# Storing a transposed activation by blocks, loading q in smaller pieces, and new due times for a hand-planned order

## The chip, the cores and the metric

The kernel runs on one core of one Trainium2 chip. The metric is the device time of one execution in microseconds (us). Before the change the median of eight runs was 908.71 us (907.18 to 910.9).

Names used here: TensorE (PE in the profile; PEld are its weight loads), VectorE (DVE), ScalarE (ACT), GpSimd (POOL), and SyncE (SP), which issues nearly all DMAs. All 16 DMA engines serve one queue here.

## The reference

Linear attention without softmax, then an MLP with softplus. All inputs are float32 in the reference; the weights arrive as 64-bit floats.

```python
kv  = einsum('bhsd,bhse->bhde', k, v)            # 8 batches, 8 heads, 576 rows, 64 wide
out = einsum('bhsd,bhde->bhse', q, kv)
rms = sqrt(mean(out * out, axis=-1) + 1e-6)
x   = (out / rms * g_norm) -> 4608 tokens x 512
h   = x @ w_in                                   # 512 -> 2048
y   = softplus(h) @ w_out                        # 2048 -> 512
```

## The kernel before, in words

**Tiles and blocks.** The 4608 tokens are 36 tiles of 128 rows; three tiles are a block of 384 tokens, so there are 12 blocks. A batch of 576 tokens is four and a half tiles.

**Attention part of a tile** (`rows`, L508): q is turned so that the head dimension lies on the partitions; `out_rows` (L521, PE) multiplies it with the batch's kv; ACT squares (L590), DVE sums by head (L525), POOL takes the power -1/2 (L528, L529), DVE scales (L533). The first two batches' q is turned by PE (L577) and copied by ACT (L584); from batch 2 on DVE turns it in 32x32 blocks (L552) from a tile `qa` that `load_q` (L413) fills with four transfers a batch (L423). `kv_of` (L473) loads k and v (L491, and the rows that are left over into `tail` tiles, L489) and multiplies them on PE (L502) in five steps a batch; ACT copies the result (L505).

**x^T.** For the first twelve tiles (`BY_PE`), PE turns the normalized x (L539) and ACT copies the result from PSUM to a tile of ring `m` (L599); SP stores it in DRAM as x^T, one tile a store, 512 rows of 512 bytes (L600). For the later tiles DVE turns x in blocks into a tile of ring `xb` (L616), and a block is stored at once in four stores (L620). The DRAM copy x^T has one tensor of 512 x 384 for each block.

**Split.** For an exact float32 product in the fast format each number is split in three parts: ACT makes the high part (L445), DVE the two others (L448, L452), into `xv`. The tiles of blocks 0 and 1 (`AT_ONCE`) are split straight from PSUM; from block 2 on `x_again` loads x^T back (L638) and splits that. The weights are converted from 64-bit words on DVE and ACT (L294 to L324) and divided in three parts as well (`divide`, L356 to L378); for the first four chunks PE makes the last remainder (L374, L375: a pair).

**MoE part.** d_ff is cut in 16 chunks of 128. A step is one chunk for one block: `mm1` (12 matmuls, L660), softplus (L682, L684) and its split (L671, L675), `mm2` (L667, three times three matmuls, one for each tile). The steps run in three phases over all 12 blocks: phase 0 takes 4 chunks for blocks 0 to 3 and 6 for the others. Partial sums go to DRAM at the end of a phase (ACT, L703; stored by L724) and come back in the next (L707, added in L709). 192 steps in all.

**The order.** Every operation is a task with an engine, a cost in ns, a due position (`pos`, in steps) and the ring places that it takes and gives back. `Plan.order` (L69) simulates engines, rings and one DMA queue and takes, engine by engine, the ready task with the smallest position among those that could start first. The program is written in that order, so each engine's order is fixed at build time; at run time each engine works through its list and waits on semaphores. While PE has nothing to do before step 6, the planner inserts filler matmuls (`warm`, L778). SP works in order as well: a store that waits for its data holds the loads behind it.

Due positions come from the list `P0` (L190): `CONVERT` and `FETCH` (when the weights of the first four chunks are converted and fetched), `EARLY` (the attention tasks, the loads of x, of partial sums) and `LATER` (the other chunks).

**Rings** (L217): `m` has 13 places, `qa` and `xb` one, `tp` one PSUM bank, `o` two. A place is free again when the last reader of its tile is done; for a stored tile that is when the store has landed.

Of the kernel before, what the change touches and what calls it, by code (L numbers as in the profile page):

```python
# [18 lines left out]
P = 128  # L19
# [21 lines left out]
class Plan:  # L41
# [15 lines left out]
    def slot(self, ring):  # L57
        return Slot(ring)

    def add(self, engine, ns, run, after=(), pos=0.0, take=(), give=(), size=0, behind=None, follows=None):  # L60
        t = Task(engine, ns, run, [a for a in after if a is not None], pos, list(take), list(give), size)
        for s in t.give:
            s.readers += 1
        self.tasks.append(t)
        t.follows = follows
        t.behind = behind
        return t
# [79 lines left out]
def kernel(  # L147
# [24 lines left out]
    nc = tc.nc  # L172
    B, H, S, D = q.shape
# [3 lines left out]
    NP = H // 2  # L177
    KD, KF = d_model // P, d_ff // P
    NT = 384
    TB = NT // P  # L180
# [6 lines left out]
    PLACES = 8  # L187
    LAST = PHASES[-1]

    P0 = [-93.0, 0.8, -33.3, -5.7, -14.1, 1.5, -43.9, 2.2, -65.0, -42.8, -62.7, -19.7, -30.7, -6.2,  # L190
          -2.2, -4.7, 2.5, -26.5, 18.0, 10.5, 5.5, 8.5, -2.0, 2.5, 3.5, 25.5, -16.5, 10.0, 6.5, 41.0,
          52.0, 65.5, 54.5, 72.0, 91.5, 94.5, 115.5, 106.0, 111.5, 8.5]
    CONVERT, FETCH, EARLY, LATER = P0[:8], P0[8:16], P0[16:27], P0[27:]
    BY_PE = 12
    AT_ONCE = 2 * TB
# [27 lines left out]
    slot, add = plan.slot, plan.add  # L223

    def new(s, shape, dtype=F32):
        if s.ring == "o":
            s.tile = o_banks[:, :, s.place]
            return s.tile
        pool = ps if s.ring in PS else sb
        s.tile = pool.tile(shape, dtype, tag=f"{s.ring}_{s.place}", name=f"{s.ring}_{s.place}")  # L230
        return s.tile
# [172 lines left out]
    xd = [dram.tile([d_model, NT], F32, name=f"x{n}") for n in range(n_blocks)]  # L404
    xb_slots = {}
    x_there = {}
# [3 lines left out]
    BL = 32  # L410
    q_slots, q_loads = {}, {}

    def load_q(b):  # L413


        q_slots[b], q_loads[b] = slot("qa"), []
        pos = x_pos(first_tile[b] + 1) - EARLY[7]

        def run(e, c):
            if not (e or c):  # L420
                new(q_slots[b], [P, NP * S])
            r0 = BL * (2 * e + c)
            nc.sync.dma_start(  # L423
                out=q_slots[b].tile[r0:r0 + BL].rearrange("j (i d) -> j i d", d=BL),
                in_=q[b, e * NP:(e + 1) * NP, :, BL * c:BL * (c + 1)].rearrange("p (i j) d -> j (p i) d", j=BL))

        for e in range(2):
            for c in range(2):
                q_loads[b].append(add("SP", 450, lambda e=e, c=c: run(e, c), (), pos + 0.2 * (2 * e + c),
                                      [q_slots[b]] if not (e or c) else [], [], 2190, behind=int(pos) - 3,  # L430
                                      follows=q_loads[b][-1] if e or c else None))

    def split(ph, t, x, ready, pos):
        n, i = divmod(t, TB)
        if i == 0:
            xv_slots[ph, n] = slot("xv")
        dst = xv_slots[ph, n]

        def cols(m, dtype=F32):
            if dst.tile is None:  # L440
                new(dst, [P, 3, KD, NT], F32R)
            return (dst.tile if dtype == F32R else dst.tile.bitcast(F32))[:, m, :, i * P:(i + 1) * P]

        def high():
            nc.scalar.activation(cols(0, F32R), x.tile, func=AF.Identity, scale=g_down)  # L445

        def low():
            nc.vector.scalar_tensor_tensor(out=cols(1, F32R), in0=x.tile, scalar=g_col, in1=cols(0),  # L448
                                           op0=ALU.mult, op1=ALU.subtract)

        def less():
            nc.vector.scalar_tensor_tensor(out=cols(2, F32R), in0=cols(1), scalar=-RADIX, in1=cols(0),  # L452
                                           op0=ALU.mult, op1=ALU.add)

        before = x_split.get((ph, n), [None])[-1:]
        a = add("ACT", 700, high, [ready] + ([] if i == 0 else [first_high[ph, n]]), pos, [dst] if i == 0 else [])
        if i == 0:
            first_high[ph, n] = a
        b = add("DVE", 740, low, [a], pos, [], [x])
        c = add("DVE", 700, less, [b], pos)  # L460
        x_split.setdefault((ph, n), []).append(c)
# [6 lines left out]
    def x_pos(t):  # L468

        n = t // TB  # L470
        return t * EARLY[0] + EARLY[1] if n == 0 else first_step[0, n] - (EARLY[2] if n == 1 else EARLY[3]) + t % TB
# [35 lines left out]

    def rows(t):  # L508
        pos = x_pos(t)
        tp, qT, o, x, r, xp, xg = (slot(n) for n in ("tp", "m", "o", "x", "r", "tp" if t < AT_ONCE else "o", "m"))  # L510

        def out_rows():

# [27 lines left out]
        def part_of_qT(n, r0):  # L541
            if qT.tile is None:
                new(qT, [P, NP, P])
            return qT.tile[:, :, r0:r0 + n]

        turned = []
        for b, r0, n, s0 in parts(t):
            if b >= 2:
                if b not in q_slots:
                    load_q(b)  # L550
                turned.append(add(
                    "DVE", 690 if n == P else 420, lambda b=b, r0=r0, n=n, s0=s0: nc.vector.transpose(  # L552
                        out=part_of_qT(n, r0),
                        in_=q_slots[b].tile.rearrange("k (p s) -> k p s", p=NP)[:, :, s0:s0 + n]),
                    q_loads[b], pos - 1, [qT] if not r0 else [], [q_slots[b]], follows=turned[-1] if turned else None))
                continue
# [17 lines left out]
            def turn_q(n=n, q_s=q_s, at_qa=at_qa, tp=slot("tp" if t < AT_ONCE else "o")):  # L574
                y = new(tp, [P, NP, P])
                for p in range(NP):
                    nc.tensor.transpose(y[:, p, :n], pairs(natural(q_s, at_qa)[:n], p), ident[:n, :n])  # L577

            tp = turn_q.__defaults__[-1]
            ld = add("SP", 900, load, (), pos - EARLY[7], [q_s] if not at_qa or t == 0 else [], [], 1220 * n // P,  # L580
                     behind=int(pos) - 3, follows=first_load[0] if t and at_qa else None)
            first_load.append(ld)
            a = add("PE", 440, turn_q, [ld], pos - 1, [tp], [q_s])
# [3 lines left out]
        a = o_task = add("PE", 640, out_rows, turned + need, pos, [o], [qT])  # L587
        for pt in parts(t):
            o_tasks.setdefault(pt[0], []).append(a)
        a = add("ACT", 600, lambda: nc.scalar.activation(new(x, [P, H, D]).rearrange("s (a k) d -> s a (k d)", k=2), o.tile, func=AF.Square,  # L590
                                                              scale=D ** -0.5), [a], pos, [x])
        a = add("DVE", 690, reduce, [a], pos, [r])
        a = add("POOL", 2300, root, [a], pos)
        a = add("DVE", 700, norm, [a, o_task], pos, [], [o, r])
        if t < BY_PE:
            a = add("PE", 440, turn_x, [a], pos + 0.5, [xp], [x])
            if t < AT_ONCE:
                split(0, t, xp, a, pos + 0.5)
            a = add("ACT", 600, lambda: nc.scalar.copy(new(xg, [P, KD, P]), xp.tile), [a], pos + 1, [xg], [xp])  # L599
            x_there[t] = [add("SP", 450, lambda: nc.sync.dma_start(  # L600
                out=x_of(t), in_=xg.tile), [a], pos + 1, [], [xg], 1000)]
            return


# [1 line left out]
        n, i = divmod(t, TB)  # L606
        g = TB if n < n_blocks - 1 else 1
        i0, i = i - i % g, i % g
        if i == 0:
            xb_slots[n] = slot("xb"), []  # L610
        xb, turns = xb_slots[n]
# [18 lines left out]
    def x_of(t):  # L630

        n, i = divmod(t, TB)
        return xd[n][:, i * P:(i + 1) * P].rearrange("(a p) t -> p a t", p=P)
# [120 lines left out]
    for c in range(KF):  # L754
        for j in (2 * c, 2 * c + 1):
            pos = CONVERT[j] if c < 4 else LATER[c - 4] + LATER[12] * (j % 2)
            weight(j, pos, FETCH[j] if c < 4 else pos)
    for b in range(B):
        kv_of(b)
        for t in range(n_tiles):  # L760
            if parts(t)[-1][0] == b:
                rows(t)
# [51 lines left out]
```

## Time and profile before

| | us |
|---|---|
| median of eight runs | 908.71 |
| the profiled execution, its own time | 909.08 |
| span of the profiled execution | 907.3 |
| PE busy | 893.4 |
| DVE busy | 624.2 |
| ACT busy | 408.1 |
| the 192 x 12 matmuls of L660 | 435.3 |
| the 192 x 9 matmuls of L667 | 433.5 |
| stores of x^T by tiles (L600), issue to landing, median of 12 | 4.1 |
| loads of q for DVE (L423), issue to landing, median of 24 | 6.8 |

The time of an execution is a little longer than its span in the trace. Busy times of different engines lie beside each other. In the page's 40 slices, one digit is the busy share of a slice of 22.7 us in tenths. In a table by windows the columns are the window, its length, then each engine's busy time with the number of its instructions, the granted TensorE clock as a share of full speed, the share of the 16 DMA engines' time that packets took, and GB/s. The chain of waits is read in order of time: start, length and what ran then; a DMA in it is a piece of time in which the engine waited for that transfer.

### The profile page before, as it was taken

The numbers are of one execution on the slowest core, as the hardware profiler recorded it, in microseconds if no ns is written. First come the engines' busy times: TensorE is split into PE (matmuls) and PEld (weight loads), VectorE is DVE, ScalarE is ACT, GpSimd is POOL, SyncE is SP. The second block draws the span as 40 slices with busy tenths as digits, with TensorE's granted clock in tenths as the row PEclk, the third lists the DMA queues.
The fourth block names the chain that finished last, engine by engine and source line by source line (L and its number), as shares of the span: only waits on it lengthen the run. The fifth ranks groups of instructions, "written<-read, shape, count | busy, mean of one in ns | idle before, by whom it ended". The sixth has DMA issues, their size and how long they took to land.

```text
span 907.3 us, 15563 instructions
## 1 busy us (share of the span) xinstructions
PE 893.4 (98%) x5983; PEld 789.0 (87%) x5983; DVE 624.2 (69%) x1054; ACT 408.1 (45%) x788; POOL 84.7 (9%) x79
## 2 busy tenths in 40 slices
PE   7989999999999999999999999999999999999998
PEld 5678888888888899998998989999899999989996
DVE  6887988676567877888668787886534555555553
ACT  4766555443444555644435454554323333333331
POOL 0443222122213200000000000000000000000000
PEclk8999999999999999999999999999999999999999
DMA  9999987579672626364334544740330433333323
GB/s 241 271 210 278 257 171 227 115 174 190 184 150 62 149 94 186 105 198 151 105 128 128 174 142 142 249 146 20 105 105 1 139 105 105 105 105 105 104 73 102
DMA packets 211451, 131.58 MB, mean 145 GB/s; under 512 B 102320, under 2 KB 185264, under 8 KB 211376
## 3 DMA queue, kind: packets, MB, share of 16 engines
q1 hardware_dynamic: 211216, 130.58, 53.0%
q8 instruction: 47, 0.77, 0.4%
q14 instruction: 28, 0.23, 0.1%
q10 hardware_dynamic: 160, 0.00, 0.0%
HBM read 91.75 MB, written 38.80 MB: 144 GB/s over the span
## 4 chain that ended last, share of the span: by engine, by line
PE 95%; DMA 3%; ACT 0%; DVE 0%; SPq 0%; issue 0%; DVEq 0%
PE h L660 45%; PE s L667 44%; DMA m<-in_v_dram 2%; PE o_banks L521 2%; PE tp L502 2%; PE h L778 1%; PE s L502 1%; DMA m<-in_k_dram 0%; PE o_banks L539 0%; PE tp L577 0%; DVE xv L448 0%; PE tp L539 0%; PE h L374 0%; SPq L491 0%; ACT m L599 0%
## 5 line engine op out<-in xcount | busy, mean ns | idle before, releaser
L660 PE MATMUL h<-xv,w 128*128 128x384 f32 x2304 | 435.3, 337 | 0.2 <-ACT w L378 0.2
L667 PE MATMUL s<-w,gv 128*128 128x512 f32 x1728 | 433.5, 395 | 0.0
L660 PEld LDWEIGHTS h<-xv,w 128*128 128x128 f32 x2304 | 406.3, 188 | 16.4 <-ACT w L378 0.4
L667 PEld LDWEIGHTS s<-w,gv 128*128 128x128 f32 x1728 | 319.8, 188 | 60.4 <-DVE gv L675 0.2
L682 ACT ACTIVATE g<-h 128x384 f32<-128x384 f32 x192 | 94.2, 491 | 401.2 <-PE h L660 399.4
L671 DVE TENSOR_TENSOR gv<-g,gv 128x384 fp32r<-128x384 f32 x192 | 106.5, 555 | 180.5 <-ACT gv L684 179.5
L684 ACT ACTIVATE gv<-g 128x384 fp32r<-128x384 f32 x192 | 100.7, 524 | 24.7 <-PE s L667 18.5
L675 DVE SCALAR_TENSOR_TENSOR gv<-gv 128x384 fp32r<-128x384 f32 x192 | 106.7, 556 | 5.8
L448 DVE SCALAR_TENSOR_TENSOR xv<-m,g_col,xv 128x512 fp32r<-128x512 f32 x102 | 76.0, 745 | 2.5 <-ACT xv L445 2.4
L452 DVE SCALAR_TENSOR_TENSOR xv<-xv 128x512 fp32r<-128x512 f32 x108 | 74.3, 688 | 2.5
L445 ACT ACTIVATE xv<-m,g_down 128x512 fp32r<-128x512 f32 x102 | 70.1, 712 | 2.9 <-DMA m<-x 2.8
L529 POOL TENSOR_TENSOR r<-r,half 128x8 f32<-128x8 f32 x36 | 66.1, 1835 | 3.0
L709 DVE SCALAR_TENSOR_TENSOR m<-s,scale,m 128x512 f32<-128x512 f32 x24 | 17.9, 747 | 29.7 <-PE s L667 29.7
L533 DVE TENSOR_TENSOR x<-o_banks,r 128x512 f32<-128x512 f32 x36 | 24.8, 689 | 18.8 <-POOL r L529 8.4
L528 POOL TENSOR_SCALAR r<-r 128x8 f32<-128x8 f32 x36 | 17.3, 480 | 216.4 <-DVE r L525 215.9
L709 DVE SCALAR_TENSOR_TENSOR m<-s,m 128x512 f32<-128x512 f32 x36 | 23.7, 685 | 7.8 <-PE s L667 7.8
L521 PEld LDWEIGHTS o_banks<-kv,m 64*64 64x64 f32 x1152 | 19.9, 134 | 9.7 <-issue 5.5
L311 ACT ACTIVATE sq<-sq,big 128x512 bf16<-128x512 bf16 x32 | 22.9, 715 | 10.7 <-DVE m L307 10.7
L359 DVE TENSOR_TENSOR m<-m,w 128x512 f32<-128x512 f32 x30 | 20.6, 687 | 10.2 <-ACT w L356 9.8
L525 DVE TENSOR_REDUCE r<-x 128x8 f32<-128x512 f32 x36 | 24.2, 678 | 4.6 <-ACT x L590 4.6
L590 ACT ACTIVATE x<-o_banks 128x512 f32<-128x512 f32 x36 | 21.1, 592 | 12.3 <-PE o_banks L521 7.0
L521 PE MATMUL o_banks<-kv,m 64*64 64x64 f32 x1152 | 24.5, 224 | 0.8 <-ACT m L584 0.7
(71 smaller groups left out, 429.7 us busy)
## 6 DMA issues: line engine op xcount, KB each, us to landing
m<-x SPq DMA_DIRECT2D x102, 256.0 KB, 4.7
part<-m SPq DMA_DIRECT2D x72, 256.0 KB, 2.6
m<-part SPq DMA_DIRECT2D x72, 256.0 KB, 4.0
raw<-in_moe_w_in_dram SPq DMA_DIRECT2D x16, 512.0 KB, 5.7
m<-in_k_dram SPq DMA_DIRECT2D x32, 256.0 KB, 5.0
m<-in_v_dram SPq DMA_DIRECT2D x32, 256.0 KB, 4.7
raw<-in_moe_w_out_dram SPq DMA_DIRECT2D x16, 512.0 KB, 5.7
qa<-in_q_dram SPq DMA_DIRECT2D x24, 288.0 KB, 6.8
```

The source lines that it names most:

```text
L445: nc.scalar.activation(cols(0, F32R), x.tile, func=AF.Identity, scale=g_down)
L448: nc.vector.scalar_tensor_tensor(out=cols(1, F32R), in0=x.tile, scalar=g_col, in1=cols(0), op0=ALU.mult, op1=ALU.subtract)
L452: nc.vector.scalar_tensor_tensor(out=cols(2, F32R), in0=cols(1), scalar=-RADIX, in1=cols(0), op0=ALU.mult, op1=ALU.add)
L521: nc.tensor.matmul(y[r0:r0 + P // 2, a, c0:c0 + D], lhsT=qT.tile[e * D:(e + 1) * D, p, r0:r0 + P // 2], rhs=kvs[b % 2][e * D:(e + 1) * D, ...
L529: nc.gpsimd.tensor_tensor(out=r.tile, in0=r.tile, in1=half, op=ALU.pow)
L660: nc.tensor.matmul(hp, lhsT=w_in.tile[:, i, kd * P:(kd + 1) * P], rhs=xv.tile[:, i, kd], start=(m == 0), stop=(m == 3 * KD - 1))
L667: nc.tensor.matmul(mine[i].tile, lhsT=gv.tile[:, m, i * P:(i + 1) * P], rhs=w_out.tile[:, m], start=(c == cs[0] and m == 0), stop=(c == cs ...
L671: nc.vector.tensor_tensor(out=gv.tile[:, 1], in0=g.tile, in1=gv.tile.bitcast(F32)[:, 0], op=ALU.subtract)
L675: nc.vector.scalar_tensor_tensor(out=gv.tile[:, 2], in0=f32[:, 1], scalar=-RADIX, in1=f32[:, 0], op0=ALU.mult, op1=ALU.add)
L682: a = add("ACT", 490, lambda: nc.scalar.activation(new(g, [P, NT]), h.tile, func=AF.Softplus, scale=1.0 + E), [a], s, [g], [h])
L684: a = add("ACT", 530, lambda: nc.scalar.activation(new(gv, [P, 3, NT], F32R)[:, 0], g.tile, func=AF.Copy, scale=DOWN), [a], s, [gv])
L709: a = add("DVE", 700, lambda: nc.vector.scalar_tensor_tensor(out=new(ot, [P, d_model]), in0=bank.tile, scalar=(scale if ph == LAST else 1. ...
```

## The change

For the first twelve tiles ACT now copies a tile's x^T into its third of a block's tile of ring `xb`, and when the third tile is copied SP stores the block at once: 512 rows of 1536 bytes. All three tiles' readers wait for that one store. `load_q` loads a batch's q in eight transfers (two of the four heads of a partition group each) instead of four; the planner's cost of one is 500 ns of SP and 1095 of the queue instead of 450 and 2190. The list of due positions has other values: among them the first four chunks' conversions, where the attention tiles of block 0 stand (`EARLY[0]`, `EARLY[1]`), kv of batch 0 (`EARLY[5]`), the loads of x (`EARLY[9]`) and of partial sums (`EARLY[10]`).

In the changed file L600 is L612, L599 is L608, L638 is L652, L660 is L674, L667 is L681, L671 and L675 are L685 and L689, L778 is L792.

```diff
-    P0 = [-93.0, 0.8, -33.3, -5.7, -14.1, 1.5, -43.9, 2.2, -65.0, -42.8, -62.7, -19.7, -30.7, -6.2,
-          -2.2, -4.7, 2.5, -26.5, 18.0, 10.5, 5.5, 8.5, -2.0, 2.5, 3.5, 25.5, -16.5, 10.0, 6.5, 41.0,
-          52.0, 65.5, 54.5, 72.0, 91.5, 94.5, 115.5, 106.0, 111.5, 8.5]
+    P0 = [-74.0, 0.3, -15.3, -11.7, -11.1, 1.5, -22.9, 2.2, -78.5, -42.8, -76.2, -17.2, -26.2, -5.2,
+          -0.2, -4.2, 1.5, -19.5, 14.0, 10.5, 5.5, 25.5, -2.0, 2.5, 3.5, 2.5, -45.5, 7.5, 6.5, 38.5,
+          52.0, 65.5, 54.5, 72.5, 91.0, 94.5, 114.5, 110.5, 111.0, 8.5]
...
-        def run(e, c):
-            if not (e or c):
+        def run(a, p):
+            if not (a or p):
                 new(q_slots[b], [P, NP * S])
-            r0 = BL * (2 * e + c)
+            e, c = divmod(a, 2)
             nc.sync.dma_start(
-                out=q_slots[b].tile[r0:r0 + BL].rearrange("j (i d) -> j i d", d=BL),
-                in_=q[b, e * NP:(e + 1) * NP, :, BL * c:BL * (c + 1)].rearrange("p (i j) d -> j (p i) d", j=BL))
-
-        for e in range(2):
-            for c in range(2):
-                q_loads[b].append(add("SP", 450, lambda e=e, c=c: run(e, c), (), pos + 0.2 * (2 * e + c),
-                                      [q_slots[b]] if not (e or c) else [], [], 2190, behind=int(pos) - 3,
-                                      follows=q_loads[b][-1] if e or c else None))
+                out=q_slots[b].tile[BL * a:BL * (a + 1), p * S:(p + 2) * S].rearrange("j (i d) -> j i d", d=BL),
+                in_=q[b, e * NP + p:e * NP + p + 2, :, BL * c:BL * (c + 1)].rearrange("p (i j) d -> j (p i) d", j=BL))
+
+        for a in range(4):
+            for p in range(0, NP, 2):
+                q_loads[b].append(add("SP", 500, lambda a=a, p=p: run(a, p), (), pos + 0.1 * (2 * a + p // 2),
+                                      [q_slots[b]] if not (a or p) else [], [], 1095, behind=int(pos) - 3,
+                                      follows=q_loads[b][-1] if a or p else None))
...
-            a = add("ACT", 600, lambda: nc.scalar.copy(new(xg, [P, KD, P]), xp.tile), [a], pos + 1, [xg], [xp])
-            x_there[t] = [add("SP", 450, lambda: nc.sync.dma_start(
-                out=x_of(t), in_=xg.tile), [a], pos + 1, [], [xg], 1000)]
+            n, i = divmod(t, TB)
+            if i == 0:
+                xb_slots[n] = slot("xb"), []
+            xb, turns = xb_slots[n]
+
+            def copy():
+                if i == 0:
+                    new(xb, [P, KD, NT])
+                nc.scalar.copy(xb.tile[:, :, i * P:(i + 1) * P], xp.tile)
+
+            turns.append(add("ACT", 600, copy, [a], pos + 1, [] if i else [xb], [xp], follows=turns[-1] if turns else None))
+            if i == TB - 1:
+                st = add("SP", 450, lambda: nc.sync.dma_start(
+                    out=xd[n].rearrange("(a p) t -> p a t", p=P), in_=xb.tile), turns, pos + 1, [], [xb], 2280)
+                for u in range(t - i, t + 1):
+                    x_there[u] = [st]
```

More of the change, by code (lines that the diff above doesn't have):

```diff
@@ L509, in rows @@
         pos = x_pos(t)
-        tp, qT, o, x, r, xp, xg = (slot(n) for n in ("tp", "m", "o", "x", "r", "tp" if t < AT_ONCE else "o", "m"))
+        tp, qT, o, x, r, xp = (slot(n) for n in ("tp", "m", "o", "x", "r", "tp" if t < AT_ONCE else "o"))
         def out_rows():
```

## The prediction

> **What bounds the kernel now.** I read the page first, then busy time by windows, then TensorE's waits, then the chain of waits between 48 and 71 us. Page:
>
> ```profile
> span 907.3 us, 15563 instructions
> PE 893.4 (98%) x5983; PEld 789.0 (87%) x5983; DVE 624.2 (69%) x1054; ACT 408.1 (45%) x788; POOL 84.7 (9%) x79
> ...
> DMA  9999987579672626364334544740330433333323
> ```
>
> TensorE (PE) is busy 98% of the span, and the DMA engines are full only in the first five slices, some 113 us. The windows (busy PE, PEld, DVE, ACT, POOL, then clock, DMA share, GB/s) say where PE is not busy:
>
> ```profile
> 0.00:40.00 40.00, 33.13 (x377) 22.60 (x377) 29.85 (x54) 23.61 (x45) 10.64 (x15) 0.91 0.96 255
> 40.00:66.00 26.00, 23.61 (x291) 19.45 (x289) 22.30 (x39) 19.04 (x39) 7.91 (x9) 1.00 1.00 224
> 66.00:98.00 32.00, 31.89 (x392) 27.15 (x389) 25.24 (x43) 18.93 (x37) 13.37 (x11) 1.00 1.03 251
> 98.00:320.00 222.00, 222.00 (x2007) 192.46 (x2007) 165.69 (x282) 105.16 (x203) 52.81 (x46) 1.00 0.72 167
> 320.00:902.80 582.80, 582.80 (x2926) 527.31 (x2924) 380.32 (x639) 241.38 (x466) 0.00 (x0) 1.00 0.39 120
> ```
>
> From 98 to 902.8 us PE never idles, so nothing there can be won, only lost. The first matmul group of the MoE part (L660) starts at 40.00; behind it PE idles 2.39 + 0.11 = 2.5 us until 98, and runs six filler matmuls of L778 (rows at 59.09, 59.91 and 71.89 us: 0.62 + 0.71 + 0.63 = 2.0). So 4.5 us is all that a better order after step 0 can recover. PE's waits and the chain say what the idle is:
>
> ```profile
> PE s L502 <- DMA m<-in_v_dram: 4.3, 3, 3.6
> PE tp L502 <- DMA m<-in_v_dram: 2.0, 2, 1.3
> ```
>
> ```profile
> 48.48 7.34 DMA m<-in_v_dram
> 55.82 0.04 issue
> 55.86 0.69 PE tp L502 x16
> ...
> 58.63 6.67 DMA m<-in_v_dram
> 65.29 0.14 issue
> 65.43 0.69 PE tp L502 x16
> 66.11 2.29 PE h L660 x12
> 68.40 0.61 PE tp L502 x16
> 69.02 0.62 PE o_banks L521 x32
> 69.64 0.58 PE tp L539 x4
> 70.22 0.70 PE s L667 x3
> ```
>
> The kernel waits for v, 6.7 to 7.3 us after its issue, while the DMA share is 1.00: **the start is a DMA queue with TensorE behind it**, the rest is TensorE. The last rows are my prices for PE: 0.62 us for a kv step (L502) and a tile's q·kv (L521), 0.45 for four transposes (L539), 0.70 for a third of L667, 2.1 for an L660 group.
>
> **The change, part by part.**
>
> *Stores of x^T.* Twelve stores of 256 KB in 512-byte rows become four of 768 KB in 1536-byte rows. The trace's DMA records from 60 to 130 us give 30.5 ns for a 512-byte packet, 52.7 for 1024, 104.4 for 2048, so some 78 for 1536. A tile cost 512 x 30.5 / 16 = 0.98 us of all 16 engines, a block will cost 512 x 78 / 16 = 2.5 instead of 2.93: 1.7 us less queue over four blocks. ScalarE (ACT) makes the same twelve copies (0.58 each). Twelve places of the 13-place ring m are no longer taken, and SP issues eight DMAs fewer.
>
> *q.* Six batches, four transfers of 288 KB each, become eight of 144 KB, with the same 128-byte packets: 9216 x 14.0 / 16 = 8.1 us of queue a batch, as before. SP issues 24 more, at least 0.46 us each (the shortest row of L423), 11 us over 210; the longest rows of L423 are 5.3 and 5.9 us, when one transfer held SP, and shorter ones let other loads in between. In the built order each SP DMA waits on one of eight semaphores in turn, last used eight DMAs earlier, so eight are in flight: eight pieces are 8 x 1.0 us of work against the 2.0 us in which the fastest store (L724) lands. I take 0; bounds -1 (the hole that one long issue leaves) to +1 (SP late once).
> A q transfer of 288 KB lands in 4.7 to 9.4 us at a full DMA share, so its fixed part is covered. The Trainium skill, "DMA: Bandwidth & Descriptors", section Bandwidth, speaks against this edit: batch transfers to 1 MiB or more. By the 2 us a transfer that its section "Anatomy of one DMA" fits for the software queue, 24 more would be 48 us, 6 with eight in flight, and the time 913.5; the full queue speaks for 0.
>
> *The due times (P0).* They set the order of every engine up to about 120 us, and here the time is decided. The first 25 rows of SP's order are equal, so both kernels stand alike up to the v load that lands at 32.15 (PE waits for it until 32.17). From there I price both queues with the records above: k and v 1.69, a weight 1.69, a tail 0.63, a tile of q 1.27, a 144 KB piece 1.01, a partial sum 0.84. Check on before: w_in of chunk 3 comes after 22.1 us of queue and landed at 54.87 (22.7 measured, x1.03); a later v after 31.3, landed 65.3 (x1.06); the last x load of block 2 after 57.4, landed 89.8 (x1.00). So my sums hold within 0 to 6%; I use 1.03.
>
> Step 0: in both orders 10 L502, 4 L521, 3 L539, 6 L577 and 3 weight pairs stand before it, and 47 against 46 fillers. The third tile's chain (L533 at 36.08, L539 at 36.91, L445, copy, L448 at 38.81, L452 until 40.28) is the same. After puts the pair of w_in chunk 2 (0.75) right ahead of it: 40.8. That pair stood earlier in before's idle; at step 2 the two orders differ by 0.2 us.
>
> Step 3 (last of block 0): in after w_in of chunk 3 stands behind 26.4 us of queue, because of four pieces of batch 2's q, block 0's store and w_out ahead of it: 32.15 + 1.03 x 26.4 = 59.3, 4.4 us later than before. From landing to the last ACT division before took 7.9 us; after has 0.4 us more of VectorE (DVE) ahead in its order and a split and a copy on ACT (1.1): 59.3 + 9.4 = **68.7** against 66.04. But by then after's PE has done two thirds of L667, two L502 and two L539 more: 1.4 + 1.24 + 0.9 = 3.5 us. Even is 69.5: after is 0.8 ahead.
>
> Block 2's first step: before at 96.4. After has three L667 thirds, one L502 and two L521 more ahead of it: 2.1 + 0.62 + 1.24 = 4.0, even is 100.4. Before spent 0.7 on the way for the fillers at 71.89 and small idles that after's order has not (its six fillers, 2.0, all stand before step 3): after comes to 98.9. Block 2's last x load is behind 62.9 us of queue: 96.9 at x1.03, ready 2.2 later (L445, L448, L452), 99.1. It just fits.
>
> *The new wait.* Ring xb has one buffer: a block's first copy waits until the previous block's store has landed. On ACT behind it stand the divisions of w_out chunk 3 and the squares of tiles 8 and 9, and on PE tile 8's and 9's L521, which need the two o banks that the uncopied tiles hold. Block 1's store is behind 40.3 us: lands 73.7. PE reaches that L521 at 68.7 + 2.1 + 0.6 + 2.1 = 73.5, and the copy takes 0.6: 0.8 late, part of which PE would wait anyway for the next v load (41.8 us of queue, 75.2). Ends 0 and 0.8; I take 0.3. Block 2's store (55.9 us, 89.7) meets the next copy at about 88 with PE's L521 1 us behind it: 0 to 1, I take 0, for two thirds of L667 stand between.
>
> Sum: -0.8 - 0.7 + 0.3 = **-1.2 us**. From block 4's first step on both PE orders have done the same work, so nothing else comes in. The profiled run is 909.08 (span 907.3 and 1.8 around it), 0.4 above the median of the eight runs: 907.9 for such a run, **907.5** on the median.
>
> **Rivals.**
> 1. *The order holds better* (17%): L667, L502 and L521 cover every DMA wait, the fillers fall into time that PE would lose anyway, and shorter issues of q close the queue's hole before 65 us. All 2.5 us idle go, with up to 1.5 of the fillers: -2.5 to -4, some 905.5. For it: 1.7 us less queue. Against: w_in chunk 3 arrives later.
> 2. *The store's landing takes over* (slower, 28%). If the queue runs at x1.06 or SP meets one more wait, block 1's store lands at 75, block 2's at 91.4, block 2's last x load at 98.8 (ready 101.0, 2.1 after PE), block 3's store (70 us of queue) at 106.4 in front of VectorE's first block turn, with a step's L671 and L675 behind it. It decides from 2 us of delay at 95 us of the span: -1.2 + 2.1 + 1 + 0.5, or about +2.4, 911. For it: DMA share 1.00 to 1.03 and a lead of 0.8 to 1.5 us only. Against: the x1.00 measured at 90 us.
> 3. *The idle only moves* (13%): w_in chunk 3 at x1.06 is 60.1, step 3 at 69.5, even; PE waits for a weight instead of v: 0 (-0.5 to +1.5), 908.7.
>
> **How the numbers follow.** Forecast 42% (-2.5 to -0.3). A measurement tells about 0.2%, 1.8 us, from no change: faster than 906.9 is rival 1 and less than half of the forecast, 0.37; slower than 910.5 is most of rival 2 and a little of 3, 0.28; the rest 0.35. The range, 905.0 to 911.3, reaches to both rivals.
>
> **What would show it.** First L660 at 40.5 to 41; step 3 at 68 to 69.5 with its releaser ACT (division), not v; PE idle between 40 and 98 under 1.5 us; no idle ahead of block 2's step; fillers again 2 us; a block's store landing in 5 to 7 us; waits of ACT on a landing store ahead of the copy (L608) under 1 us. Wrong if PE idles after 98 us, if L608 waits 2 us or more, or if the first L660 starts after 42.

## The result, and the profile after

The changed kernel takes 911.35 us (median of 11 runs, 910.92 to 914.16) against 908.42 for the kernel before on the same chip (30 runs): a ratio of 1.0035, 95% interval 1.0028 to 1.0043. It is slower by about 3 us. Its profiled execution took 911.53 us, 2.45 more than that of before.

The page of the changed kernel:

```profile
span 909.7 us, 15578 instructions
PE 894.2 (98%) x5982; PEld 788.5 (87%) x5982; DVE 625.9 (69%) x1054; ACT 409.2 (45%) x788; POOL 82.3 (9%) x79
...
DMA  9999889479682535355333435651330433433323
```

The same windows as for before (length, then busy PE, PEld, DVE, ACT, POOL, clock, DMA share, GB/s):

```profile
0.00:40.00 40.00, 31.82 (x374) 21.82 (x374) 29.27 (x53) 23.20 (x44) 8.85 (x15) 0.91 1.00 254
40.00:66.00 26.00, 25.10 (x309) 20.09 (x308) 20.99 (x36) 17.23 (x36) 7.82 (x7) 1.00 0.99 234
66.00:98.00 32.00, 31.03 (x372) 25.81 (x369) 26.28 (x45) 22.10 (x45) 11.77 (x12) 1.00 1.07 263
98.00:320.00 222.00, 220.43 (x2000) 190.71 (x1999) 166.84 (x281) 102.96 (x196) 53.89 (x47) 1.00 0.71 163
320.00:902.80 582.80, 582.80 (x2929) 528.04 (x2928) 379.36 (x638) 243.72 (x470) 0.00 (x0) 1.00 0.39 120
```

TensorE's idle time between 40 and 66 us fell from 2.39 to 0.90 us. In its place stand 0.97 us between 66 and 98 (0.11 in before), and 1.57 after 98, where before had none. What TensorE waited for has changed too:

```profile
PE o_banks L521 <- DVE x L533: 0.9, 1, 0.9
PE o_banks L577 <- ACT x L590: 0.9, 1, 0.9
...
PE o_banks L521 <- ACT xb L608: 0.7, 1, 0.7
...
PE o_banks L539 <- DVE x L533: 0.5, 1, 0.5
```

The 2.0 us on v (row `PE tp L502` of before) are gone. All but the last of the rows shown are waits at `o_banks`, the PSUM tile that holds both places of ring `o`; the last, L539 behind L533, waits for the x that it turns. The longest stretch stands right ahead of block 2's first step; the chain of waits there reads:

```profile
98.80 0.45 PE o_banks L539 x4
99.25 0.02 issue
99.27 0.59 ACT xb L608
99.87 0.04 issue
99.91 0.74 PE o_banks L521 x32
100.65 0.02 issue
100.67 0.60 ACT x L590
...
101.37 0.70 DVE x L533
102.07 0.04 issue
102.11 0.69 PE o_banks L521 x32
```

TensorE turns tile 11 (L539), ACT copies it out of its place (L608), TensorE can write tile 13 into that place (L521), ACT squares it (L590), VectorE divides tile 12 (L533), which frees the other place, and TensorE writes tile 14 (L521). Six operations of three engines, one after the other, with no transfer among them. Block 2's first step follows at 102.74.

To see what was lost where, I compared the starts of the 192 steps in both traces and took off the difference in the work that TensorE had done by then. After is 0.64 us late at step 0; 0.06 at step 6; 0.63 at step 7; 2.53 at step 8, which is block 2's first; 3.0 from step 16 to the last step (the end itself is 2.5 late, because what follows the last step is 0.6 shorter). From step 0 to step 16 both kernels do exactly the same work on TensorE (192 matmuls of the first product, 135 of the second, 448 of L521 and so on): 98.93 us before, 101.29 after. Of these 2.36 us, 0.94 are more idle time; 1.42 are rows of the same work taking longer until the next one starts, above all the 36 matmuls of L539 (3.91 to 4.58) and the 135 of L681 (33.19 to 33.68). For L539 the traces show why: the 27 transposes that another one follows take 3.16 us in before and 3.17 in after; the nine that end a tile go from 0.76 to 1.41. A row of a step or a filler starts 0.03 us after the last transpose has started, L521, L502 or L577 0.11 us or more after it, and one of those three follows six times in after and three times in before. So this part, too, is the order.

### The profile page after: what moved, and what is told of

Its sections match the earlier page's. It is cut to its first block, busy times and chain, and to the rows that moved or that the text cites. A ratio compares the mean times of both kernels' runs of the same rounds, so it can differ in the third digit from the quotient of the medians.

```text
span 909.7 us, 15578 instructions
## 1 busy us (share of the span) xinstructions
PE 894.2 (98%) x5982; PEld 788.5 (87%) x5982; DVE 625.9 (69%) x1054; ACT 409.2 (45%) x788; POOL 82.3 (9%) x79
## 4 chain that ended last, share of the span: by engine, by line
PE 96%; DMA 2%; ACT 1%; DVE 0%; issue 0%; SPq 0%; DVEq 0%
PE s L681 45%; PE h L674 45%; PE o_banks L521 2%; PE tp L502 2%; DMA m<-in_v_dram 1%; PE h L792 1%; DMA m<-in_q_dram 1%; PE s L502 1%; DMA tail<-in_k_dram 0%; PE o_banks L539 0%; DVE x L533 0%; PE tp L577 0%; PE h L374 0%; PE tp L539 0%; PE o_banks L577 0%
## 5 line engine op out<-in xcount | busy, mean ns | idle before, releaser
L674 PE MATMUL h<-xv,w 128*128 128x384 f32 x2304 | 435.0, 337 | 0.0
L681 PE MATMUL s<-w,gv 128*128 128x512 f32 x1728 | 434.9, 395 | 0.0
L674 PEld LDWEIGHTS h<-xv,w 128*128 128x128 f32 x2304 | 406.5, 188 | 15.9
L681 PEld LDWEIGHTS s<-w,gv 128*128 128x128 f32 x1728 | 319.5, 188 | 60.6 <-DVE gv L689 0.2
L685 DVE TENSOR_TENSOR gv<-g,gv 128x384 fp32r<-128x384 f32 x192 | 106.5, 555 | 180.9 <-ACT gv L698 179.5
L689 DVE SCALAR_TENSOR_TENSOR gv<-gv 128x384 fp32r<-128x384 f32 x192 | 106.9, 557 | 5.9
L529 POOL TENSOR_TENSOR r<-r,half 128x8 f32<-128x8 f32 x36 | 65.1, 1809 | 3.0
L533 DVE TENSOR_TENSOR x<-o_banks,r 128x512 f32<-128x512 f32 x36 | 24.7, 686 | 15.3 <-POOL r L529 6.9
L521 PEld LDWEIGHTS o_banks<-kv,m 64*64 64x64 f32 x1152 | 19.9, 134 | 11.5 <-issue 5.8
L590 ACT ACTIVATE x<-o_banks 128x512 f32<-128x512 f32 x36 | 21.1, 593 | 14.9 <-PE o_banks L521 6.5
L521 PE MATMUL o_banks<-kv,m 64*64 64x64 f32 x1152 | 24.6, 224 | 2.4 <-DVE x L533 0.9
```

What stands on the lines that cost most here:

```text
L521: nc.tensor.matmul(y[r0:r0 + P // 2, a, c0:c0 + D], lhsT=qT.tile[e * D:(e + 1) * D, p, r0:r0 + P // 2], rhs=kvs[b % 2][e * D:(e + 1) * D, ...
L529: nc.gpsimd.tensor_tensor(out=r.tile, in0=r.tile, in1=half, op=ALU.pow)
L674: nc.tensor.matmul(hp, lhsT=w_in.tile[:, i, kd * P:(kd + 1) * P], rhs=xv.tile[:, i, kd], start=(m == 0), stop=(m == 3 * KD - 1))
L681: nc.tensor.matmul(mine[i].tile, lhsT=gv.tile[:, m, i * P:(i + 1) * P], rhs=w_out.tile[:, m], start=(c == cs[0] and m == 0), stop=(c == cs ...
L685: nc.vector.tensor_tensor(out=gv.tile[:, 1], in0=g.tile, in1=gv.tile.bitcast(F32)[:, 0], op=ALU.subtract)
L689: nc.vector.scalar_tensor_tensor(out=gv.tile[:, 2], in0=f32[:, 1], scalar=-RADIX, in1=f32[:, 0], op0=ALU.mult, op1=ALU.add)
```

## The experiments

The theories, as the expectations name them: **A**, the store by blocks costs, through its one buffer; **B**, the due times cost, or fit only one combination; **C**, q in eight pieces costs or gains. **D** came later: any order other than that of before costs some microseconds. A ratio is to the kernel before, timed on the same chip in the same session, with its 95% interval.

### One part of the change at a time

Each kernel is the one before with one part of the diff alone (`f_store`, `f_q`, `f_due`), or with both data edits and the old due times (`f_data`). `g_no_store` and `h_no_q` are the changed kernel without one data edit. The edits in short:

```diff
 f_store  + xb.tile[:, :, i*P:(i+1)*P] / one store a block      (rest as before)
 f_q      + for a in range(4): for p in range(0, NP, 2)          (rest as before)
 f_due    + P0 = [-74.0, 0.3, -15.3, ...]                        (rest as before)
 f_data   - P0 = [-74.0, ...]   + P0 = [-93.0, ...]              (rest as after)
 g_no_store  - one store a block   + one store a tile            (rest as after)
 h_no_q      - for p in range(0, NP, 2)   + for c in range(2)    (rest as after)
```

> The kernel before with the block stores of x^T alone (old q transfers, old due times). Theory A, the one-buffer ring: a block's copies are ordered behind the landing of the store before, the turned tiles hold the two o banks and the next tiles' L521 start late: 910.5 to 912, PE idle of 1.5 us or more between 85 and 110 us. Theory B, the due times make the loss: 907.5 to 909.5. Theory C, the q pieces make it: as before, 908 to 909.

> The kernel before with q in eight pieces a batch alone. Theories A and B: within 1 us of before, 907.5 to 909.5. Theory C: 910.5 to 912.

> The kernel before with the new due times alone: stores by tiles from ring m, q in four transfers. Theory A: within 1 us of before or faster, since a copy waits for no store. Theory B: 910.5 to 912, with step 3 at about 71 us as in the changed kernel. Theory C: as A.

> The changed kernel with the old due times: block stores and q pieces. Theory A: 910.5 to 912. Theory B: 907.5 to 909.5. Theory C: 910.5 to 912.

> The changed kernel without the block stores: q in eight transfers and the new due times, x^T stored by tiles as before. Theory A (the store costs the 3 us): 907 to 909. Rival B (the due times fit only with the block store, which frees twelve places of ring m and saves queue time): 912 to 916, near the 914.4 of the due times alone.

> The changed kernel with q in four transfers as before: block stores in the one-buffer ring and the new due times. If the due times fit the block store, it comes near the changed kernel: 910 to 913. If they fit only both edits together, as the run without the block store suggests: 914 to 920.

| | due times of before | new due times |
|---|---|---|
| no data edit | 908.42 | `f_due` 914.42, 1.0072 [1.0045, 1.0099] |
| q in eight | `f_q` 909.07, 1.0006 [0.9991, 1.0021] | `g_no_store` 915.78, 1.0077 [1.0054, 1.0099] |
| stores by blocks | `f_store` 922.79, 1.0154 [1.0118, 1.0191] | `h_no_q` 913.31, 1.0060 [1.0038, 1.0082] |
| both | `f_data` 917.50, 1.0097 [1.0066, 1.0128] | after 911.35, 1.0035 [1.0028, 1.0043] |

Of the first four runs only `f_q` lies in a range that a theory gave for it; `f_store`, `f_due` and `f_data` lie above all of theirs. `g_no_store` is in B's range, `h_no_q` between its two (four runs, 911.3 to 915.8). TensorE's order in `h_no_q` is that of after, row by row, and its interval overlaps after's, so these runs don't show that q in eight pieces is worth anything beside the other two parts.

No part is worth a fixed sum: the store by blocks costs 14 us with the old due times and, with the new ones, saves 4 beside q in eight (915.78 to 911.35). The new due times cost 6 us alone and save 6 beside both data edits. So B holds in this form: what the due times cost or save depends on the edits beside them. `f_q` shows a second thing. At step 3 it is 2.7 us ahead of before, with the difference in work taken off, and the lead is gone between steps 26 and 27, where the chain of waits of `f_q` has batch 5's last piece:

```profile
186.23 5.31 DMA qa<-in_q_dram
...
191.83 0.46 DVE m L552
192.29 0.04 issue
192.33 1.29 PE o_banks L521 x62
```

VectorE waits for that piece to land, and TensorE for VectorE.

### Is it the one buffer?

The weights of chunks 6 and 7 have places of 6 KB a partition, the size of `xb`, and are not there yet while blocks 0 to 3 are stored. First, each of the four blocks takes such a place, and the planner makes its own order for it (the lines that matter):

```diff
-    BY_PE = 12
+    BY_PE, OWN = 12, ["w0_6", "w1_7", "w0_7", "w1_6"]
...
-                xb_slots[n] = slot("xb"), []
+                xb_slots[n] = slot(OWN[n]), []
```

> The kernel before with block stores only (922.8 us with the one-buffer ring), but each of the first four blocks has a buffer of its own: the places of the weights of chunks 6 and 7, which are free until chunk 6 and 7 are converted late in phase 0. Theory A (the ring of one buffer makes the loss: a copy waits until the block before has landed, and behind it ACT, the o banks and PE): the loss goes, 907 to 910. Rival B (the loss is the store itself: tiles become readable only when the third is copied, and 512 rows of 1536 bytes go out in one burst): still 918 to 923.

> The changed kernel, with four buffers for the first four blocks as in the run beside it. Theory A: the 1.9 us that the chain of copies on the o banks costs between 94 and 103 us go, and some of the 3 us stays away: 908 to 909.5. Rival B (the due times were fitted to the one-buffer ring, so a different ring leads the planner to another order that fits no better): 910 to 914.

> The kernel before with both data edits (block stores and q in eight transfers), the old due times, and a buffer of its own for each of the first four blocks. With one buffer it took 917.5 us. Theory A (the ring of one buffer makes most of that): 908 to 911. Rival (two changes of order add up): 913 to 917.

Measured: `g_store_own` 910.64 (1.0030 [1.0015, 1.0045]) against 922.79 with one buffer; `h_data_own` 912.19 (1.0051 [1.0032, 1.0071]) against 917.50; `g_all_own` 910.32 (1.0023 [1.0012, 1.0033]) against 911.35. The one buffer makes 12 of `f_store`'s 14 us, more than half of `f_data`'s 9 and perhaps 1 of after's 3 (there the intervals overlap). `g_store_own` is 0.6 over A's range, `h_data_own` between its two ranges, `g_all_own` in B's. For the first two that reads as A, but it doesn't say how. So the second pair keeps the planner's order for one buffer, instruction by instruction, and only writes to the other memory, so that no copy can wait for a landing store:

```diff
                 if i == 0:
-                    new(xb, [P, KD, NT])
+                    xb.tile = sb.tile([P, 3, d_model], F32R, tag=OWN[n], name=OWN[n])
```

> The changed kernel with its order unchanged on every engine, but the first four blocks are written to memory of their own (the places of the weights of chunks 6 and 7), so no copy waits for a landing store. If the wait for the one buffer at run time makes the 3 us: 908 to 909.5. If it is the order that the planner built around the one buffer (the copy of a turned tile put behind the store, the o bank held meanwhile): 910.5 to 911.5, no gain.

> The kernel before with block stores only, in the order that took 922.8 us with the one-buffer ring, but with memory of its own for each of the first four blocks. With this order kept, a wait at run time for the buffer would be gone: 911 to 915 if that wait was the cost (a copy waited 2.1 us there, and TensorE up to 7 us). If the order is the cost: 919 to 923; the planner's own order for four buffers took 910.6.

Measured: `i_all_order_kept` 912.11 (1.0037 [1.0024, 1.0050]), no different from after. `i_store_order_kept` 921.38 (1.0135 [1.0112, 1.0157]), no different from `f_store`, where ACT's waits had one row for the buffer:

```profile
ACT xb L608 <- DMA x<-xb: 2.1, 1, 2.1
```

That wait is gone in `i_store_order_kept`. Its median is 1.4 us lower, with overlapping intervals, and its trace is 2.4 us shorter from step 0 to step 16 (110.21 against 112.60), so the wait can have cost `f_store` some 2 us. **The rest of the loss, some 11 us, is the order that the planner builds around the buffer:** with the same edit and the same memory, its order for four buffers takes 910.64. In after no row of ACT waits for a landing store at all, so `i_all_order_kept` had no wait to remove, and its time stays. A as a wait at run time falls as the main cost.

### The data edits in the order of before

Here every engine keeps the order of before. `h_q_same_order` issues each of q's transfers as two halves; `i_both_order_of_before` also stores blocks 0, 1 and 3 whole, from memory of their own (two loads of block 2 stand ahead of its last store in SP's order, so block 2 stays with tiles). The edits, shortened:

```diff
+            for p in range(0, NP, 2): nc.sync.dma_start(
+                out=q_slots[b].tile[r0:r0 + BL, p * S:(p + 2) * S]..., in_=q[b, e * NP + p:e * NP + p + 2, ...]...)
...
+        elif not left[n]:      # the block's third tile
+            nc.sync.dma_start(out=xd[n].rearrange("(a p) t -> p a t", p=P), in_=xt_of(whole[n]))
```

> The kernel before with its own order on every engine, each of the four transfers of a batch's q issued as two of 144 KB one behind the other. It takes the size of the pieces apart from the other order that they lead the planner to. If the pieces themselves win (a long issue no longer holds SP): 905.5 to 907.5, and step 3 before 65 us. If only the order made the 2.6 us of the run with q in eight pieces: 908 to 909.5.

> The order of the kernel before on every engine, with q's transfers issued in halves (907.6 alone) and with blocks 0, 1 and 3 stored whole from memory of their own; block 2 stays with stores by tiles, because two of its loads stand before its last store. Saves 1.3 us of queue over three blocks. If the data edits by themselves are good and only orders were bad: 906 to 907.6, the fastest here. If the whole block's burst of 1.9 us in the queue delays v or w_in: 908 to 910.

Measured: 907.58 (0.9988 [0.9979, 0.9998]) and **906.31 (0.9973 [0.9963, 0.9983])**, 2.5 us under the kernel before of its session (908.80) and 5 under the changed kernel's 911.35. This version beats both. Two windows of `i_both_order_of_before`, and the first three rows of its TensorE waits:

```profile
40.00:66.00 26.00, 25.59 (x304) 21.44 (x303) 22.94 (x40) 19.18 (x39) 8.45 (x8) 1.00 0.95 213
66.00:98.00 32.00, 31.89 (x388) 26.86 (x387) 26.60 (x45) 20.58 (x40) 12.75 (x11) 1.00 1.03 264
```

```profile
PE s L502 <- DMA m<-in_v_dram: 4.0, 2, 3.4
PE h L799 <- DVE ident_r L767: 1.6, 1, 1.6
PE o_banks L521 <- ACT m L584: 0.7, 3, 0.3
```

The idle time of before between 40 and 66 us is down from 2.39 to 0.41, the row `PE tp L502 <- DMA m<-in_v_dram`, second of before, has gone (2.0 us there, 0.3 with q's halves alone; what is left of waits on v lies ahead of step 0), and nothing comes back later: from step 0 to step 16 it takes 96.80 us for the same work (98.93 before), 97.16 with q's halves alone. Of the 1.3 us between the medians of these two, the traces show 0.36 in this stretch as the block stores' part.

### How much does any other order cost?

`h_cost_900` changes one number that only the planner sees; `g_q_234` leaves batches 5 to 7 in four transfers (shortened).

```diff
-                out=x_of(t), in_=xg.tile), [a], pos + 1, [], [xg], 1000)]
+                out=x_of(t), in_=xg.tile), [a], pos + 1, [], [xg], 900)]
```

```diff
+        k = 2 if b in {2, 3, 4} else NP
+            for p in range(0, NP, k):
```

> The kernel before with one number changed that only the planner sees: the queue time of a tile's store of x^T, 900 ns instead of 1000. The same instructions and data, another order. Theory D (the due times fit one order only, so any other order costs some microseconds whatever the reason for it): 910 to 916. Rival (orders that the same due times give are alike to 1 us): 907.5 to 909.5.

> The kernel before with q in eight transfers for batches 2, 3 and 4 and in four for 5 to 7. Theory C (eight pieces win 2.6 us at the start, because the issue of a long transfer no longer holds SP; the 3.0 us lost at 177 to 198 us are batch 5's, whose eight pieces stand behind partial sums and x loads in SP's order): the gain is kept, 905.5 to 906.5. Rival (the early gain is given back wherever PE next meets the queue, at batch 6 or 7 if not at 5): 908 to 909.

Measured: 908.71 (1.0008 [0.9999, 1.0018]) and 908.06 (0.9996 [0.9985, 1.0008]). D in its strong form falls: the one other order that this cost brings loses some 0.7 us, 1.6 at most by the interval. `g_q_234` lies in its rival's range: it gives its lead back at the same place as `f_q`, waiting for batch 5 in four pieces, so it is not their size. It is their place among SP's issues: before issues half of batch 5's q ahead of three loads of x, `f_q` and `g_q_234` a quarter, and the last piece lands at 191.54 and 191.59 us against 188.79 in before. In `h_q_same_order`, with the halves in the places of before, it lands at 188.60, and TensorE doesn't wait there.

### The chain ahead of block 2

The last run tests the reading of the chain above. In the changed kernel two places are exchanged, nothing else:

```diff
 VectorE:  - L533, L448, L452     + L448, L452, L533       (ahead of block 2's first step)
 TensorE:  - L521, L674 (step 8)  + L674 (step 8), L521
```

> The changed kernel with two places of its order exchanged by hand, all else as it was: VectorE takes the split of the third tile of block 2 (L448, L452) ahead of the division L533 that waits for a square, and TensorE takes block 2's first step ahead of the last L521 in front of it. If the chain copy, L521, square, L533, L521 at 99 to 102.7 us is what lasts of the loss: the step starts at 101.1 to 101.8 instead of 102.7, and the time is 909.6 to 910.4. If another wait comes late right behind it (the copies and squares that the same chain delays): 911 to 912.

Measured: 910.50 (1.0017 [1.0008, 1.0026]), 0.85 us less than after (1.6 by the ratios, whose intervals just miss each other) and 0.1 over the range that the chain's theory gave. Step 8 begins at 100.34 us in an execution that was 0.81 ahead of after from step 0 on, so at 101.15 by after's start. The chain there is now:

```profile
97.99 0.45 PE o_banks L539 x4
98.44 0.02 issue
98.47 0.59 ACT xb L608
99.06 0.04 issue
99.10 0.69 PE o_banks L521 x32
99.80 0.61 PE tp L502 x16
100.41 2.29 PE h L674 x12
102.70 0.62 PE o_banks L521 x32
```

The step covers the square and the division, and the last L521 finds its place free. The 0.7 us behind the copy L608 remain, as they should. From step 0 to step 16 TensorE's idle time is 2.55 us, as in before, and the stretch takes 100.56.

## Why the prediction was wrong, point by point

- **What bounds the kernel**: right. Of the 3.0 us by which after is late at its last step, 2.4 come between step 0 and step 16, and 2.0 of the 2.5 us idle could be recovered: `i_both_order_of_before` did.
- **Queue and stores of x^T**: right. The w_in of chunk 3 landed at 59.2 (59.3 predicted); block 1's and 2's stores landed at 72.4 and 88.0 (73.7 and 89.7), 3.8 and 4.7 us after their issue. A packet of 1536 bytes took 79.8 ns in the mean (78 estimated). Block 2's last x load landed at 94.79, earlier than the 96.9 predicted.
- **q at 0, between -1 and +1**: the halves in before's order give -1.8 us from step 0 to step 16 (-1.1 counted from the span's start, since step 0 came 0.7 later) and some 0.7 to 1.1 by the medians and the ratio. So the end -1 was the one to take, but not for "the hole that one long issue leaves": around 49 and 59 us SP issues two transfers of q one behind the other and is held 6.51 and 5.78 us in before, and by their four halves 6.37 and 6.12. What changed is that the two loads of v on which TensorE waited landed 1.1 us earlier each (54.71 for 55.82, 64.22 for 65.29); no run shows why. The Trainium skill, "DMA: Bandwidth & Descriptors", speaks against small transfers in its section Bandwidth, and the price of its section "Anatomy of one DMA" put 24 more of them at 913.5 by the prediction's estimate; `h_q_same_order` issues 24 more and took 907.58.
- **Step 0 at 40.8**: 40.64.
- **Step 3 at 68.7**: 71.14. The weight came in time, but ACT's square of tile 7 waited 2.2 us for a place of ring `x` that L539 had still to free (`ACT x L590 <- PE o_banks L539`), and tile 7's division and L539 stand ahead of the step. Of this, all is made up by step 6, so it isn't what lasts.
- **Block 2's first step at 98.9**: 102.74. *This is the step that failed.* Its working added up TensorE's work and the landing of the last x load. The loads were in time: the last landed at 94.79, and ACT split them from 96.20 without waiting. What was late is the chain on the two places of `o_banks`, which no term of the sum priced, though the paragraph on the new wait named "the two o banks that the uncopied tiles hold". TensorE stood still there for 0.68 and 0.90 us, after lost 1.9 us against before between step 7 and this step, and with two places in the order exchanged the step began at 101.15 by after's start. The lead of 0.8 at step 3 did not come either. That work between two steps is the same in sum does not say that it can be done without waiting: rows that hand the same two places on are a chain across TensorE, ACT and VectorE. The prediction's own sign of being wrong came, too: TensorE idles 1.57 us after 98.
- **The new wait, 0.3**: 0. No copy waited for a landing store, and taking the buffer away in the same order changes nothing.
- **"From block 4's first step on both PE orders have done the same work, so nothing else comes in"**: half right. No idle time comes in, but for the same work the rows took 1.42 us more up to there: 0.66 at the last transposes of tiles, by what follows them, and 0.49 at L681, which no run takes apart.
- **Rival 2** named about 911, on the right side, for a wrong reason: the landing did not take over. Its price and the measured one agree by accident.

What stays open: `g_all_own` is still 2 us over before with four buffers, and the swaps leave 1.5. It is no longer idle time: from step 0 to step 16 TensorE idles 1.90 and 2.55 us there (2.50 in before), but the stretch takes 100.27, with two fillers more, and 100.56 (98.93). No run here takes that part further apart.

## What to carry to other kernels

Where a planner or a list of due times sets the order, an edit to the data and the new order that it brings are two changes: make the edit in the old order first. Here the order decided, for nearly the same data edits, between 2.5 us won and 3 us lost. And when rows move, don't sum only busy time and transfers; follow each small ring (two PSUM places, two buffers of x) through the moved rows, and ask which places share a tile: the chain here ran one engine at a time.

## What the runs showed of the hardware

**The granted clock fell to half after a stretch in which TensorE was only partly idle.** Windows of `f_store`, cut where the clock changes (busy PE is the first column, the clock the third from the end):

```profile
58.20:61.70 3.50, 1.66 (x28) 1.21 (x30) 3.43 (x7) 1.34 (x3) 0.00 (x0) 1.00 0.92 140
61.70:65.10 3.40, 2.72 (x23) 2.21 (x20) 2.28 (x4) 1.12 (x2) 0.00 (x0) 0.51 0.96 167
65.10:68.60 3.50, 3.50 (x40) 2.63 (x40) 0.04 (x1) 1.86 (x4) 0.00 (x0) 0.50 0.84 247
...
102.70:106.10 3.40, 1.12 (x7) 0.61 (x6) 3.37 (x6) 2.43 (x4) 3.15 (x4) 1.00 1.11 246
106.10:109.50 3.40, 1.34 (x34) 0.94 (x32) 2.63 (x5) 1.07 (x2) 0.64 (x1) 0.50 0.52 183
109.50:112.90 3.40, 3.23 (x39) 3.12 (x40) 2.88 (x6) 0.11 (x1) 2.40 (x2) 0.50 0.94 287
```

Within a trace all changes of the clock lie on one grid of 3.41 us. After a stretch of the grid in which TensorE was busy less than about half (0.33 to 0.51, once 0.56), the clock was half for one to three stretches; after 0.54 or more it otherwise stayed, and once, in `g_no_store`, after 0.46. In `f_store` the longest single idle time was 2.3 us. In the four half-clock stretches TensorE was busy 10.8 us; if that work takes half as long at full clock, up to 5 of the 13 us by which this span (920.3) is longer than before's are the clock's, an estimate. `f_due`'s executions go the same way: the three with a mean clock of 0.998 took 913.94 to 914.23 us, the one with 0.989 took 919.14, which does not tell cause from effect. By the estimate the clock makes a bad order worse. Neither before nor after fell that low from 40 us on (lowest 0.62 and 0.74). The Trainium skill, "TensorE: Matmul & The Clock Gate", Part 1, gives the drop "after ≥1 idle window (~3.4µs)"; the grid agrees, but the runs show that half a window idle is enough.

**Two readers of one PSUM tile took turns.** VectorE's division of tile 12 began (101.37) when ACT's square of tile 13 ended, though it needs only tile 12's place. VectorE's row in the changed kernel:

```profile
101.37 0.69 DVE L533 TENSOR_TENSOR x<-o_banks,r 128x512 f32<-128x512 f32 x1 [1.05 <-ACT x L590]
```

Both places lie interleaved in the one tile `o_banks`. The Trainium skill, "PSUM — Partial Sum Buffer", section "PSUM bank collisions raise a hardware error", says that engines must not use one bank at the same time; here the program keeps them apart with a wait of 1.05 us. Tile 12's factor was ready at 98.89 (the end of L529 on POOL) and VectorE free at 100.32; had the division begun then, it would have ended before TensorE was through with L502 at 101.15, so by these rows most of the 0.90 us ahead of the last L521 is this link's. TensorE is kept off in the same way: L577 waited 0.88 us, until 57.82, for the square of tile 6, though it can't write to that tile's place, since tile 6 was divided only at 61.26. That a tile for each place would avoid it wasn't tried.

**The first 40 us vary.** `f_q` and `g_q_234` have the same TensorE order up to there, and their first steps began at 40.02 and 41.59. So differences of one profiled execution under 1.6 us before step 0 say nothing, and the stretches above are counted from step 0.
